# Two chained mixtures behind packed attention: the second mixture's weight sums placed later, its first output weights decoded earlier

## The chip, the cores and the metric

One core of a Trainium2 chip runs the whole program in one launch. The metric is device time in microseconds (us), lower is better. The time before is 807.88 us, the median of 3 runs (807.45 to 808.22).

## The reference

Inputs are q, k, v of shape (4, 8, 576, 64) and p of shape (4, 8, 32, 64), and two pairs of weights, `w_in` (512 x 2048) and `w_out` (2048 x 512).

```python
def sm_attn(qq, kk, vv):
    s = scale * np.matmul(qq, kk.transpose(0, 1, 3, 2))
    a = np.exp(s - np.max(s, axis=-1, keepdims=True))
    a = a / (np.sum(a, axis=-1, keepdims=True) + 1e-09)
    return np.matmul(a, vv)
p_packed = sm_attn(p, k, v)
x = sm_attn(q, p_packed, p_packed)           # as 2304 tokens x 512
h = x @ moe_w_in;  x = (h * np.tanh(softplus(h))) @ moe_w_out
h = x @ moe2_w_in; out = np.where(h > 0, h, np.exp(h) - 1) @ moe2_w_out
```

The result is 2304 x 512. The weights arrive as 64-bit numbers, so that each of them has to be decoded on the chip from two 32-bit words.

## The kernel before

Every large product is made from a high and a low part of each operand (`split_hi` on ScalarE, `split_lo` on VectorE), three matmuls for one. The engines are TensorE (PE), VectorE (DVE), ScalarE (ACT), GpSimd (POOL, here a DMA queue) and SyncE (SP, the other DMA queue). An engine works in the order in which the program gives it its instructions; outside the startup a planner orders them for each engine by its own estimate of when they are ready, with the order of the Python program as the priority. Buffers come from pools with a fixed number: `slot` (28), `small` (9), `wo` (2), `dec` (3), `sg` (2, for raw weights of the second mixture and for two of the four `yr` tiles).

**Startup.** Attention of the first two batches and the first two blocks (0 to 31) of the first mixture, in an order written out by hand.

**First mixture**, `mixture1` (L1062), iterations `i` from 32 to 129. An iteration has `gemm1(i)` (L657, six matmuls of 288 columns), `mish(i)` (L672: `t` on ACT, `gh` on ACT, `gl` on DVE) and `gemm2(i - 2)` (L691, twelve matmuls, which needs that `gl`). Into these are woven:
- the attention of batches 2 and 3, one step or two an iteration. Batch 2 starts with iteration 35, batch 3 with 65, and that of batch 3 takes some 23 iterations and the folds that come between. `packed` (L477) makes `pv` on DVE, which PE transposes; scores go through ACT's exponent (`e`);
- the folds (L625) of the packed keys into `w_in`, four for each batch, for batch 3 in iterations 87 to 92;
- the weight sums of the second mixture, `combine` (L273). That mixture's first layer is multiplied with seven products in place of eight, and for this sums and differences of the quarters of `w_in` are made ahead. There are eight `combine`s of 28 steps: two raw tiles are loaded (512 KB each on SP) and decoded (`s0` on ACT, three DVE instructions, L214, L224, L230, into `dec`), four sums are made on DVE (L282), and then there are seven pairs: `hi` on ACT into a tile `w2c` (L257), `lo` on DVE (L265) and two DMAs of 128 KB on POOL to `w2_dr` in HBM (L314), `w_dr` in the trace. The tile `w2c` comes from the two `wo` buffers and is free when both of its DMAs have landed.

`STG=(34, 110)` spreads the 224 steps evenly over iterations 34 to 109, 2.95 an iteration. At `Y0 = 114` four `yr` tiles (the tokens, from HBM) are loaded by twelve DMAs, and 36 steps of the tokens' sums (`y_steps`, L742) are spread over iterations 115 to 127. In iterations 127 to 129 the first six products of the second mixture are started.

**Second mixture**, `mixture2` (L1148): three passes over 768 tokens, each of eight quartets. A quartet (L816) has seven `product`s (L790, six matmuls of 384 columns, with `w2c` read back from HBM three tiles ahead), an ELU for four results on ACT and DVE, and four `gemm4` (L868) of nine matmuls of 512 columns. `gemm4` needs `w_out` decoded as `w2oh` and `w2ol`: for the first two quartets rows 0 to 3, for the next two rows 4 to 7, and so on. A decoding has six steps: `s0` on ACT (L194), three on DVE, `s4` on ACT (`w2oh`, L257) and `s5` on DVE (`w2ol`, L265). Before, all sixteen of them are made in `mixture2`: two ahead of its loop by `tick(14)`, then three steps behind each product in the first pass (four in the last quartet of a pass).

Of the kernel before, what the change touches and what calls it, by code (L numbers as in the profile page):

```python
# [10 lines left out]
F32R = mybir.dt.float32r  # L11
# [16 lines left out]
    EXPS=(0, 1, 2, 3, 4, 5, 6, 7, 8, 9, 10, 11, 12, 23, 24, 25, 26),  # L28
    LOW=(2, 4, 7, 9, 10, 11, 12, 13, 14, 15, 16, 17, 19, 22, 29, 30, 31),
    HALVED=True,  # L30
    STG=(34, 110),
    Y0=114,
    AHEAD=3,
)

# [31 lines left out]
def kernel(  # L67
# [202 lines left out]
        split_hi(val, hi, factor)  # L270
        split_lo(val, hi, lo, factor)

    def combine(c, p):  # L273

        tiles = [decode("w2i", 2 * p + x, c) for x in range(2)]
        d = {}

        def cut(x, h):
            return tiles[x][1]().bitcast(F32)[:, 256 * h:256 * h + 256]

        def op(out, a, b, alu):
            nc.vector.tensor_tensor(out=out(), in0=a(), in1=b(), op=alu)  # L282

        def s1():
            d["s"] = dp.tile([128, 512], I32, tag="dec", name="sums").bitcast(F32)
            op(lambda: d["s"][:, 0:256], lambda: cut(0, 1), lambda: cut(1, 1), ALU.add)

        def s2():
            op(lambda: d["s"][:, 256:512], lambda: d["s"][:, 0:256], lambda: cut(0, 0), ALU.subtract)

        def s3():
            op(lambda: cut(0, 1), lambda: cut(0, 0), lambda: cut(0, 1), ALU.subtract)

        def s4():
            op(lambda: cut(1, 0), lambda: cut(1, 0), lambda: d["s"][:, 256:512], ALU.subtract)

        vals = [
            lambda: cut(0, 0), lambda: d["s"][:, 256:512], lambda: cut(1, 0), lambda: d["s"][:, 0:256],
            lambda: cut(0, 1), lambda: cut(1, 0), lambda: cut(1, 1),
        ]  # L300

        def parts(x):
            def view():
                return vals[x]().rearrange("p (i n) -> p i n", i=2)

            def hi():
                d[x] = wo.tile([128, 2, 2, 128], F32R, tag="wo", name="w2c")
                split_hi(view(), d[x][:, :, 0, :], 1.0 / WSCALE)

            def lo():  # L310
                split_lo(view(), d[x][:, :, 0, :], d[x][:, :, 1, :], 1.0 / WSCALE)
                for i in range(2):
                    n = (2 * c + i) * 7 + x
                    nc.gpsimd.dma_start(out=w2_dr[n // 2][:, n % 2, p], in_=d[x][:, i].bitcast(F32))  # L314

            return [hi, lo]

        st = tiles[0][0] + tiles[1][0] + [s1, s2, s3]
        for x in range(7):
            if x == 5:  # L320
                st.append(s4)
            st += parts(x)
        return st
# [721 lines left out]
    class Track:  # L1045
# [11 lines left out]
        def start(self, i):  # L1057
            if not self.cur and self.q and self.q[0][0] <= i:
                self.cur = deque(self.q.popleft()[1])
                self.cur.popleft()()  # L1060

    def mixture1():  # L1062
        att, fol = Track(), Track()

        def whole(f):
            return [f[0], lambda: [f[i]() for i in (1, 3, 2, 4)]]

        at = {}
        dec = deque()
        for b in range(1, B):  # L1070
            i0 = (b - 1) * 2 * NK
            if b > 1:
                for st_ in attention_steps(b):
                    att.q.append((i0 + (3 if b == 2 else 1), st_))
                for x in range(2):
                    at.setdefault(max(i0 - 2 + 2 * x, 2 * NK), []).append(lambda b=b, x=x: load_kt(k, kt_in, b, x, "k"))
            for c in range(4):
                if b > 1 or c >= P["F1"]:
                    fol.q.append((max(i0 + NK + 4 * c + P["FOLDOFF"][c], 2 * NK), whole(fold(b, c))))
                    at.setdefault(max(i0 + NK + 4 * c + P["RELOFF"], 2 * NK), []).append(lambda c=c: reload_w1i(c))  # L1080
        w2q = deque()
        for c in range(4):
            for p_ in range(2):
                w2q.append(((2 * p_, c), (2 * p_ + 1, c)))
        cur = deque()
        ahead = deque(t for g in w2q for t in g)

        def step_w2():
            if not cur and w2q:
                if len(ahead) == 16:  # L1090
                    for _ in range(2):
                        load_raw("w2i", *ahead.popleft())
                (r, c), _ = w2q.popleft()
                st = combine(c, r // 2)
                for n in (4, 9):
                    if ahead:
                        st.insert(n, lambda t=ahead.popleft(): load_raw("w2i", *t))
                cur.extend(st)
            if cur:
                cur.popleft()()  # L1100

        for i in range(2 * NK, NA + LAG):
            for f in at.get(i, ()):
                f()
            fol.posts()
            att.posts()
            if not fol.cur and not att.cur:
                fol.start(i)
            if i < NA:
                gemm1(i)  # L1110
                for f in mish(i):
                    f()
            if 48 <= i < 64:
                att.posts()
                if not fol.cur and not att.cur and not fol.due(i):
                    att.start(i)
            for f in gemm2(i - LAG):
                f()
            if not fol.cur and not att.cur:
                fol.start(i)  # L1120
            if not fol.cur and not att.cur and not fol.due(i):
                att.start(i)
            u0, u1 = P['STG']
            if u0 <= i < u1:
                n = 8 * 28
                for _ in range((i + 1 - u0) * n // (u1 - u0) - (i - u0) * n // (u1 - u0)):
                    step_w2()
            if i == u1:
                while cur or w2q:
                    step_w2()  # L1130
            if i == P['Y0']:
                for k_ in range(4):
                    load_y(0, k_)
                ys = deque(f for st in y_steps(0) for f in st)
                n_y = len(ys)
            if P['Y0'] < i < NA:
                n = n_y * (i - P['Y0']) // (NA - 1 - P['Y0'])
                while len(ys) > n_y - n:
                    ys.popleft()()
            if i >= NA - 1 and not steps:  # L1140
                st, groups = quartet(0, 0)
                steps.extend(st)
                first.extend(groups)
            if i >= NA - 1:
                for _ in range(2):
                    steps.popleft()()

    def mixture2():  # L1148
        w2o = [4 * c + r for c in range(4) for r in (0, 2, 1, 3)]
        load = deque(w2o)  # L1150
        todo = deque()
        for _ in range(2):
            load_raw("w2o", load.popleft(), 0)

        def refill():
            r, d = w2o.pop(0), []

            def step(i):
                if not d:
                    d.extend(decode("w2o", r, 0))  # L1160
                d[i]()

            todo.extend(lambda i=i: step(i) for i in range(6))
            if load:
                todo.append(lambda r=load.popleft(): load_raw("w2o", r, 0))

        def tick(n):
            while n and todo:
                todo.popleft()()
                n -= 1  # L1170

        for _ in range(2):
            refill()
        tick(14)
        for _ in range(2):
            refill()
        ready = deque()
        for j in range(3):
            for q in range(NQ):
                lastq = q == NQ - 1 and j < 2  # L1180
                if j == 0 and q in (0, 2, 4):
                    for _ in range(4):
                        refill()
                if q == 0 and j == 0:
                    st, groups = list(steps), list(first)
                else:
                    st, groups = quartet(j, q)
                if j < 2 and q == NQ - 2:
                    for k_ in range(4):
                        load_y(j + 1, k_)  # L1190
                    ys = y_steps(j + 1)
                    todo.extend(ys[0] + ys[1])
                done = 7 - len(st)
                for x in range(7):
                    if x >= done:
                        st[x - done]()
                    if lastq and x < 5:
                        todo.extend(ys[x + 2])
                    if x in (0, 2, 4, 6):
                        if x == 6:  # L1200
                            ready.append(groups[0])
                        if ready:
                            gemm4(*ready.popleft())
                    tick(4 if lastq else 3)
                ready.extend(groups[1:])
        while ready:
            gemm4(*ready.popleft())
# [37 lines left out]
```

## Time and profile before

| | |
|---|---|
| median of 3 runs | 807.88 us |
| profiled execution, its own time | 809.47 us |
| its span | 807.5 us |
| PE busy | 758.6 us (94%) |
| PE loading weights | 676.5 us (84%) |
| DVE busy | 534.1 us (66%) |
| ACT busy | 398.0 us (49%) |
| mean granted PE clock | 0.973 |

The profile shows one execution, in microseconds from the start of its span. An engine that is not the bound may idle at no cost; what counts is where PE stops, what ended its stop, and at which clock it works. "<-" names the releaser of a wait: the instruction or the DMA that ended it. A DMA has an issue (the time that its queue needs for it) and a landing (from the issue to the arrival of the data). Iteration 32 of the loop begins at 126.96 us, iteration 84 at 292.73, 96 at 328.86, 112 at 369.12 and 117 at 380.95; the last block's `gemm1` ends at about 405.10 us, and at 444.00 the second mixture runs on without stops. Cutting the windows there gives the stretches of the change.

### The profile page before, as it was taken

What the parts mean: (1) busy time and instruction counts of PE and PEld (TensorE: products, weight loads), DVE (VectorE), ACT (ScalarE), POOL (GpSimd) and SP (SyncE); (2) the same over time, 40 slices, a digit from 0 to 9 for tenths busy, and PEclk for the clock granted to TensorE, in tenths of its full rate; (3) what the DMA queues carried; (4) which work ended last, traced back from release to release, by engine and by line L of the source; (5) the groups of instructions that cost most, each with busy time, mean ns of one, the idle gap of its engine ahead of it and who ended that gap; (6) DMA issues with size and microseconds to landing.
All of it is one profiled execution on the core that took longest, in us unless ns stands there. A gap on an engine that the chain in (4) does not pass through costs nothing.

```text
span 807.5 us, 14023 instructions
## 1 busy us (share of the span) xinstructions
PE 758.6 (94%) x5237; PEld 676.5 (84%) x5237; DVE 534.1 (66%) x1134; ACT 398.0 (49%) x840; POOL 76.0 (9%) x145
## 2 busy tenths in 40 slices
PE   6399999986999899999987999999999999999997
PEld 4198898875888898999976989888899999888986
DVE  5999977553974579565357988686446667454644
ACT  2899734562764547545444544354223345322323
POOL 1100001222133223321000000000000000000000
PEclk9599999998999999999997999999999999999999
DMA  8998455667356654472245526455443437443412
GB/s 296 413 365 264 125 151 227 208 174 223 130 169 236 165 183 162 150 235 96 105 175 184 192 79 207 132 200 163 147 115 120 117 106 227 138 130 106 126 57 78
DMA packets 79299, 138.80 MB, mean 172 GB/s; under 512 B 38528, under 2 KB 46720, under 8 KB 79232
## 3 DMA queue, kind: packets, MB, share of 16 engines
q1 hardware_dynamic: 69984, 112.55, 43.7%
q0 software_dynamic: 7808, 23.60, 7.8%
q10 hardware_dynamic: 1440, 1.77, 0.7%
q8 instruction: 41, 0.67, 0.3%
q14 instruction: 26, 0.21, 0.1%
HBM read 109.58 MB, written 28.31 MB: 171 GB/s over the span
## 4 chain that ended last, share of the span: by engine, by line
PE 67%; DVE 10%; ACT 9%; DMA 8%; issue 4%; SPq 1%; POOL 0%; ACTq 0%; DVEq 0%
PE h L799 19%; PE o L879 7%; PE o L880 7%; PE o L881 7%; PE acc L703 5%; PE acc L705 5%; DMA w_dr<-w2c 5%; PE acc L704 5%; PE h L667 3%; PE h L668 2%; PE h L669 2%; PE pm L633 1%; DMA yr<-y_dr 1%; ACT t L677 1%; DVE dec L224 1%
## 5 line engine op out<-in xcount | busy, mean ns | idle before, releaser
L799 PE MATMUL h<-y,w2c 128*128 128x384 f32 x1008 | 199.1, 339 | 4.6 <-ACT hs L376 3.4
L799 PEld LDWEIGHTS h<-y,w2c 128*128 128x128 f32 x1008 | 180.7, 189 | 16.4 <-ACT hs L376 3.8
L703 PE MATMUL acc<-gh,w1oh 128*128 128x288 f32 x512 | 151.3, 301 | 2.9 <-DVE y L378 2.0
L705 PE MATMUL acc<-gh,w1ol 128*128 128x288 f32 x512 | 152.4, 299 | 0.0
L704 PE MATMUL acc<-gl,w1oh 128*128 128x288 f32 x512 | 152.3, 299 | 0.1
L879 PE MATMUL o<-w2oh,gh 128*128 128x512 f32 x288 | 114.6, 399 | 4.6 <-ACT w2oh L257 3.9
L880 PE MATMUL o<-w2ol,gh 128*128 128x512 f32 x288 | 113.5, 394 | 0.0
L703 PEld LDWEIGHTS acc<-gh,w1oh 128*128 128x128 f32 x512 | 96.8, 191 | 10.7 <-issue 6.7
L881 PE MATMUL o<-w2oh,gl 128*128 128x512 f32 x288 | 102.2, 395 | 0.0
L705 PEld LDWEIGHTS acc<-gh,w1ol 128*128 128x128 f32 x512 | 97.7, 191 | 3.5 <-issue 3.4
L704 PEld LDWEIGHTS acc<-gl,w1oh 128*128 128x128 f32 x512 | 97.8, 191 | 3.0 <-issue 1.8
L685 DVE TENSOR_TENSOR gl<-t,gh 128x288 fp32r<-128x288 f32 x128 | 57.2, 451 | 44.7 <-ACT gh L376 43.6
L667 PE MATMUL h<-a2h,gh 128*128 128x288 f32 x256 | 78.2, 306 | 5.8 <-ACT t L677 4.5
L677 ACT ACTIVATE t<-h 128x288 f32<-128x288 f32 x128 | 50.9, 403 | 52.6 <-PE h L669 52.3
L668 PE MATMUL h<-a2l,gh 128*128 128x288 f32 x256 | 76.3, 299 | 0.0
L669 PE MATMUL h<-a2h,gl 128*128 128x288 f32 x256 | 76.1, 299 | 0.0
L314 POOL DMA_DIRECT2D w_dr<-w2c x112 | 60.0, 541 | 164.1 <-DVE w2c L265 156.2
L257 ACT ACTIVATE gh<-t 128x384 fp32r<-128x384 f32 x96 | 50.1, 523 | 47.9 <-DVE t L810 46.5
L879 PEld LDWEIGHTS o<-w2oh,gh 128*128 128x128 f32 x288 | 54.6, 190 | 15.0 <-ACT w2oh L257 4.2
L263 DVE TENSOR_TENSOR gl<-t,gh 128x384 fp32r<-128x384 f32 x96 | 52.9, 553 | 15.2 <-ACT gh L257 14.7
L880 PEld LDWEIGHTS o<-w2ol,gh 128*128 128x128 f32 x288 | 54.6, 190 | 9.7 <-DVE w2ol L265 0.2
L376 ACT ACTIVATE gh<-t 128x288 fp32r<-128x288 f32 x112 | 49.4, 443 | 26.0 <-PE acc L705 23.9
(128 smaller groups left out, 1050.5 us busy)
## 6 DMA issues: line engine op xcount, KB each, us to landing
w2c<-w_dr SPq DMA_DIRECT2D x84, 512.0 KB, 3.7
w_dr<-w2c POOLq DMA_DIRECT2D x112, 128.0 KB, 2.6
w1r<-w_dr SPq DMA_DIRECT2D x24, 512.0 KB, 6.6
raw_w1i<-in_moe_w_in_dram SPq DMA_DIRECT2D x16, 512.0 KB, 10.7
raw_w1o<-in_moe_w_out_dram SPq DMA_DIRECT2D x16, 512.0 KB, 9.3
raw_w2i<-in_moe_w_in_dram SPq DMA_DIRECT2D x16, 512.0 KB, 4.4
raw_w2o<-in_moe_w_out_dram SPq DMA_DIRECT2D x16, 512.0 KB, 3.4
y_dr<-y POOLq DMA_DIRECT2D x16, 288.0 KB, 2.8
```

Of the source, the lines that this page charges most:

```text
L314: nc.gpsimd.dma_start(out=w2_dr[n // 2][:, n % 2, p], in_=d[x][:, i].bitcast(F32))
L667: nc.tensor.matmul(out=hp, lhsT=wh, rhs=xh, start=(kt == 0), stop=False)
L668: nc.tensor.matmul(out=hp, lhsT=wh, rhs=xl, start=False, stop=False)
L669: nc.tensor.matmul(out=hp, lhsT=wl, rhs=xh, start=False, stop=(kt == 1))
L677: nc.scalar.activation(out=d["t"], in_=d["h"], func=ACTF.Mish)
L703: nc.tensor.matmul(out=o, lhsT=wh[:, cs], rhs=gh, start=first, stop=False)
L704: nc.tensor.matmul(out=o, lhsT=wh[:, cs], rhs=gl, start=False, stop=False)
L705: nc.tensor.matmul(out=o, lhsT=wl[:, cs], rhs=gh, start=False, stop=last)
L799: nc.tensor.matmul(out=hp, lhsT=w[:, p, a, :], rhs=y[:, b, :], start=start and p == 0 and i == 0, stop=p == 1 and i == 2, skip_group_check ...
L879: nc.tensor.matmul(out=o, lhsT=gh[:, ts], rhs=wh, start=(n == 1), stop=False)
L880: nc.tensor.matmul(out=o, lhsT=gh[:, ts], rhs=wl, start=False, stop=False)
L881: nc.tensor.matmul(out=o, lhsT=gl[:, ts], rhs=wh, start=False, stop=(n == NK))
```

## The change

The even spread becomes two: 70 steps over iterations 32 to 83, and 154 over iterations 84 to 111 (5.5 an iteration). The third number of a stretch is its steps. In the second stretch `w2c` comes from the nine `small` buffers, two pairs sharing one tile, in place of the two `wo` buffers. The first group of `w_out` (rows 0, 2, 1, 3) is loaded and decoded from iteration 112 on, 28 steps at six an iteration; the tokens' sums start with `Y0 = 117` and are spread over 118 to 127. The other three groups are queued with quartets 0, 2 and 4 as whole groups, and two steps in place of three follow each product.

```diff
-    STG=(34, 110),
-    Y0=114,
+    STG=((32, 84, 70), (84, 112, 154)),
+    W0=112,
+    Y0=117,
...
-    def combine(c, p):
+    def combine(c, p, late):
...
             def hi():
-                d[x] = wo.tile([128, 2, 2, 128], F32R, tag="wo", name="w2c")
+                if not late:
+                    d[x] = wo.tile([128, 2, 2, 128], F32R, tag="wo", name="w2c")
+                else:
+                    if x % 2 == 0:
+                        d["w"] = small([128, 2, 2, 2, 128], F32R, "w2c")
+                    d[x] = d["w"][:, x % 2]
                 split_hi(view(), d[x][:, :, 0, :], 1.0 / WSCALE)
...
+    todo = deque()
+
+    def second(c):
+        rows = [4 * c + r for r in (0, 2, 1, 3)]
+        for r in rows[:2]:
+            todo.append(lambda r=r: load_raw("w2o", r, 0))
+        for x, r in enumerate(rows):
+            d = []
+
+            def step(i, r=r, d=d):
+                if not d:
+                    d.extend(decode("w2o", r, 0))
+                d[i]()
+
+            todo.extend(lambda i=i, step=step: step(i) for i in range(6))
+            if x < 2:
+                todo.append(lambda r=rows[x + 2]: load_raw("w2o", r, 0))
+
+    def tick(n):
+        while n and todo:
+            todo.popleft()()
+            n -= 1
...
-            u0, u1 = P['STG']
-            if u0 <= i < u1:
-                n = 8 * 28
-                for _ in range((i + 1 - u0) * n // (u1 - u0) - (i - u0) * n // (u1 - u0)):
-                    step_w2()
-            if i == u1:
+            for u0, u1, n in P['STG']:
+                if u0 <= i < u1:
+                    for _ in range((i + 1 - u0) * n // (u1 - u0) - (i - u0) * n // (u1 - u0)):
+                        step_w2(u0 > 2 * NK)
+            if i == P['STG'][-1][1]:
                 while cur or w2q:
-                    step_w2()
+                    step_w2(True)
+            if P['W0'] <= i < P['Y0']:
+                if i == P['W0']:
+                    second(0)
+                tick(28 // (P['Y0'] - P['W0']) + 1)
             if i == P['Y0']:
+                tick(28)
                 for k_ in range(4):
                     load_y(0, k_)
...
     def mixture2():
-        w2o = [4 * c + r for c in range(4) for r in (0, 2, 1, 3)]
...
-        for _ in range(2):
-            refill()
-        tick(14)
-        for _ in range(2):
-            refill()
...
                 if j == 0 and q in (0, 2, 4):
-                    for _ in range(4):
-                        refill()
+                    second(q // 2 + 1)
...
-                    tick(4 if lastq else 3)
+                    tick(4 if lastq else 2)
```

## Rows read from the trace of the kernel before

**Rows 1.** Busy time by stretch: length, PE, PEld, DVE, ACT, POOL, PE clock, DMA share, GB/s.
```profile
126.96:292.73 165.77, 152.02 (x1367) 133.83 (x1366) 98.95 (x224) 88.68 (x203) 41.31 (x77) 0.97 0.57 179
292.73:328.86 36.13, 36.13 (x315) 31.88 (x314) 32.82 (x72) 23.62 (x50) 9.72 (x19) 1.00 0.55 186
328.86:369.12 40.26, 39.45 (x307) 38.22 (x305) 20.41 (x46) 20.18 (x50) 14.24 (x27) 1.00 0.55 185
369.12:380.95 11.83, 11.83 (x92) 11.83 (x91) 5.72 (x13) 6.16 (x16) 1.17 (x3) 1.00 0.32 117
380.95:405.10 24.15, 24.15 (x185) 24.15 (x185) 10.70 (x24) 12.45 (x30) 0.00 (x0) 1.00 0.23 88
405.10:444.00 38.90, 31.09 (x151) 27.47 (x150) 26.07 (x50) 17.31 (x32) 1.08 (x2) 0.87 0.52 185
```

**Rows 2.** Waits of PE from 126.96 to 405.10: total, times, longest.
```profile
PE pm L517 <- DVE pv L500: 4.0, 1, 4.0
PE h L667 <- ACT t L677: 3.9, 6, 1.2
PE pm L460 <- ACT e L433: 3.0, 2, 2.1
PE acc L703 <- DVE y L378: 2.0, 1, 2.0
PE acc L703 <- ACT gh L376: 0.9, 1, 0.9
PE pm L411 <- ACT e L433: 0.4, 1, 0.4
```

**Rows 3.** Timeline of ACT, then DVE, near 190 us: start, length, instruction, idle before.
```profile
190.54 0.42 ACT L257 ACTIVATE w2c<-dec 128x256 fp32r<-128x256 f32 x1 [3.77 <-DMA w_dr<-w2c]
...
190.99 0.42 DVE L265 SCALAR_TENSOR_TENSOR w2c<-dec,w2c 128x256 fp32r<-128x256 f32 x1 [5.31 <-ACT w2c L257]
```

**Rows 4.** Waits of ACT from 126.96 to 405.10, the row of the writes.
```profile
ACT w2c L257 <- DMA w_dr<-w2c: 37.4, 16, 3.8
```

**Rows 5.** Tile `w2c` in 127 to 370 us, last line in 292.73 to 328.86.
```profile
L314 POOL DMA_DIRECT2D w_dr<-w2c x112: 539/539/702, 136.5 to 368.7; - x112
...
DMA to landing us min/median/max: 2.0/2.6/10.6
...
DMA to landing us min/median/max: 2.0/2.4/4.5
```

**Rows 6.** Timeline of ACT, DVE and SP: a `t`, its `gl`, the loads `yr`.
```profile
396.30 0.41 ACT L677 ACTIVATE t<-h 128x288 f32<-128x288 f32 x1 [1.49 <-PE h L669]
...
397.22 0.46 DVE L685 TENSOR_TENSOR gl<-t,gh 128x288 fp32r<-128x288 f32 x1 [1.92 <-ACT gh L376]
...
346.16 6.92 SPq L739 DMA_DIRECT2D yr<-y_dr  x12
```

**Rows 7.** Waits of PE from 405 to 445.
```profile
PE o L879 <- ACT w2oh L257: 3.9, 1, 3.9
PE h L799 <- ACT hs L376: 3.4, 1, 3.4
```

**Rows 8.** Busy time in the four stretches of half clock, columns as in rows 1.
```profile
194.16:200.98 6.82, 5.57 (x23) 5.54 (x23) 2.21 (x5) 0.02 (x1) 2.13 (x4) 0.50 0.38 141
269.25:272.66 3.41, 3.41 (x16) 3.41 (x15) 2.95 (x7) 1.90 (x5) 0.00 (x0) 0.50 0.61 96
422.85:429.67 6.82, 5.14 (x12) 4.04 (x13) 4.78 (x9) 2.93 (x5) 0.00 (x0) 0.50 0.63 241
439.92:443.33 3.41, 3.27 (x11) 2.77 (x10) 3.32 (x6) 2.20 (x5) 0.00 (x0) 0.50 0.70 227
```

**Rows 9.** DVE on tile `dec` by stretch: length, busy (x), PE clock, DMA share, GB/s.
```profile
126.96:369.12 242.16, 57.71 (x120) 0.98 0.57 181
292.73:328.86 36.13, 12.98 (x27) 1.00 0.55 186
405.10:444.00 38.90, 15.30 (x26) 0.87 0.52 185
```

More of the change, by code (lines that the diff above doesn't have):

```diff
@@ L1086, in mixture1, with step_w2 @@
         ahead = deque(t for g in w2q for t in g)
-        def step_w2():
+        def step_w2(late):
             if not cur and w2q:
@@ L1093, in step_w2 @@
                 (r, c), _ = w2q.popleft()
-                st = combine(c, r // 2)
+                st = combine(c, r // 2, late)
                 for n in (4, 9):
@@ L1148, in mixture2 @@
     def mixture2():
-        w2o = [4 * c + r for c in range(4) for r in (0, 2, 1, 3)]
-        load = deque(w2o)
-        todo = deque()
-        for _ in range(2):
[L1153 to L1170, printed above, removed]
-        for _ in range(2):
-            refill()
-        tick(14)
-        for _ in range(2):
-            refill()
         ready = deque()
```

## The prediction

> **What bounds the kernel now.** I read first the windows of the middle of the run, cut at iterations of the first mixture's loop, to see how much of each stretch TensorE (PE) works [rows 1]. In iterations 32 to 83 PE is busy 152.02 of 165.77 us at a mean clock of 0.97; from 84 to 127 it hardly idles; at the hand-over to the second mixture it is busy 31.09 of 38.90 us at 0.87. So PE is the bound, and what can be won lies in two places: iterations 32 to 83 and the hand-over. VectorE (DVE) shows the other side: 32.82 of 36.13 us busy in iterations 84 to 95, half busy in 96 to 111, 10.70 of 24.15 us in 117 to 127.
>
> Second, PE's own waits in the loop [rows 2]: 14.2 us. The longest, 4.0 us for `pv` of the attention, is followed back in two rows [rows 3]: DVE, which makes `pv`, stood 5.31 us at the low part of a weight sum; that waited for ScalarE (ACT), which had stood 3.77 us until an earlier write of such a sum had landed. ACT did that 16 times, 37.4 us in all [rows 4]: there are two `wo` buffers, and each is free only when two POOL issues of 539 ns and their landing (2.0 to 10.6, median 2.6 us) are over [rows 5]. A burst of sums goes at 224/76 = 2.95 steps an iteration, and two sums are four steps: a buffer comes round every 1.36 iterations of 2.38 us (1.92 + 0.46 between two `gl` [rows 6]) = 3.2 us. Low part, issues and landing take 0.4 + 1.1 + 2.6 = 4.1 us. So ACT must wait.
>
> Third, the hand-over: PE idles 3.9 us for the first `w2oh` and 3.4 us for `hs`, which stands on ACT behind four more weight decodings [rows 7]. Last, the clock: four stretches at 0.5, that is 1.2 GHz, each after such a stop [rows 8].
>
> **The change, part by part.** The sum is made against the profiled execution, 809.47 us (span 807.5), 1.6 us above the median of 807.88.
>
> *Early sums thinned out.* By iteration 84 the old plan issues 50 x 2.95 = 147 steps, the new one 70. At 70/52 = 1.35 steps a buffer comes round every 4/1.35 x 2.38 = 7.1 us, against the 4.1 us above; even a landing of 5 us is met. Of the waits of [rows 2] I put 4.0 (`pv`), 2.0 (`y`), 0.9 (`gh`), 0.4 (the scores) and half of the 3.9 (`t`, made by the same ACT queue) to those landings: 9.3, of which I take 8.7. To decodings that stood on DVE ahead of the attention's maximum I put 3.0 (`e`) and a quarter of `t`: 4.0, and with half the steps half stays, 2.0 won. The last quarter of `t` stays. Clock: PE worked 5.57 us in the stretch at 194 us, which costs 2.8; the stop before it goes, so all of that. The stretch at 269 us costs 3.41/2 = 1.7; its stop is of the decoding kind, so half, 0.85. **Won: 8.7 + 2.0 + 2.8 + 0.9 = 14.4** (bounds 4, if the attention's own chain is what holds, and 17.8, if everything goes).
>
> *First weights decoded ahead.* The four decodings for the first quartets leave the hand-over. The idles of 3.9 and 3.4 us go, and the half clock, where PE worked 5.14 and 3.27 us [rows 8], gives back 2.6 + 1.6. That is 11.5. Late next: the second group's decodings, 14 steps in program order before the seventh product, on the same DVE. The first `gemm4` needs none of them, so I leave 1.5 us. **Won: 10.0** (bounds 2 and 11.5). Two steps a product in place of three afterwards: the 28 steps of a group fill its 14 products exactly; I cost it at nothing, covered by those products; uncovered, the first `gemm4` of the next group would wait one decoding.
>
> *Sums behind the last attention.* DVE pays 57.71 us for 120 instructions on `dec` [rows 9], and 16 low parts from `sums` at 0.42 [rows 3]: 64.4 us, 8.0 for each of the eight sums. In iterations 84 to 95 the old run did 12.98 us on `dec` [rows 9] and 3 x 0.42, 14.2 us of it; 12 x 5.5 = 66 steps of 28 are 2.36 sums, 18.9 us. DVE then needs 32.82 + 4.7 = 37.5 of 36.13 us. This is the tight place. What queues behind a late DVE instruction is `gl`, for which `gemm2` waits. Slack: `t` starts when PE releases it, `gl` ends 1.38 us later [rows 6], `gemm2` comes two iterations (4.76 us) later: 3.4 us. The excess and half of DVE's idle, 1.4 + 1.7 = 3.1 us, fit just so; I charge 2.0 (bounds 0 and 7). In 96 to 111 DVE takes the rest, 3.14 sums or 25.2 us, in place of some 10 of its 20.41: 36 of 40.26, no cost. POOL issues 14 x 0.54 = 7.5 us a sum, 5.5 sums or 42 us in 76; it is free for that. The late tiles come from the nine `small` buffers; the attention takes its `x` and `a2t` there until about iteration 92, and behind an allocation that waits for a landing of 2.4 us [rows 5] stands again DVE. That lies within the bound of 7.
>
> For these writes the row shows no sign of a busy DVE: in iterations 84 to 95, with DVE at 32.82 of 36.13 us, they land in 2.0 to 4.5, median 2.4 us [rows 5], against 2.6 in the loop as a whole. The Trainium skill, SBUF — State Buffer, section "SBUF: two separate sides", speaks against the change here: while DVE runs an instruction in a mode with both ports, GpSimd cannot write the descriptors of a DMA that it issues. The trace does not bear it out; by it the denser stretch would lose what rival 4 works out, 7 us.
>
> *Four decodings in iterations 112 to 116.* They cost DVE 4 instructions each, 15.30/26 x 4 = 2.35 us [rows 9], so 9.4; with the 5.72 there now (an upper bound, since some of it is tokens' sums that move on) 15.1 of 11.83 us: 3.3 over, about the slack. I charge 1.0 (bounds 0 and 3.3). *Tokens' sums start at 118, not 115.* SP's twelve loads of `yr` take 6.92 us to issue [rows 6], and the first two tiles can be loaded only when the raw weights have left their two buffers; before, they were issued at 346.16 us, long before iteration 114 (112 begins at 369.12). ACT may then stand at a `y` with `t` behind it: I charge 1.5 (bounds 0 and 4); from 117 on DVE has 13 us free. **Lost: 2.0 + 1.0 + 1.5 = 4.5.**
>
> Sum: 14.4 + 10.0 - 4.5 = 19.9. The profiled execution would be 789.6, the median **788.0 us**.
>
> **The rivals.**
> 1. *DVE becomes the bound behind the last attention.* No slack absorbs anything: 4.7 in 84 to 95 (its idle of 3.3 stays), 3.3 in 112 to 116, 2.5 for low parts that wait for ACT in between, one half-clock stretch 1.7: 12.2 in place of 4.5 with the loads' stop left out, so 24.4 - 12.2 = 12.2: 795.7 us. For it: 32.82 of 36.13. Against: PE did not stop there at all.
> 2. *The attention's waits stay*, since its own chain (scores, exponent, transposes) is as long as before. 4 won in place of 14.4: 9.5, 798.4 us. Against: [rows 3].
> 3. *The change does not do what it says*: the planner orders every engine, and the decodings may slip back behind the tokens' sums. The hand-over gives 2: 11.9, 796.0 us.
> 4. *POOL's writes are held up by DVE.* Each issue waits for one DVE instruction, 15.30/26 = 0.59 us [rows 9]: 14 x 1.13 = 15.8 us a sum against 76.4/5.5 = 13.9 that are there, so writes are 10.5 us late by iteration 112 and hold buffers that the decodings want; less the slack of 3.4, 7 us: 12.9, 795.0 us. Against: [rows 5]. The Trainium skill's page named above would have it so.
> 5. *Rivals 1 and 2 together*: 4 + 10 - 12.2 = 1.8: 806.1 us, at the edge of what can be told.
> 6. *Slower.* What moves is 77 steps, 77/28 x 8.0 = 22.0 us, and 9.4 us of decoding: 31.4 us of DVE work between iterations 84 and 116. If PE waits for all of it, since `gl` is queued behind it and `gl` is on PE's path, that is 31.4 against 24.4 won: 814.9 us. It decides from 24.4/31.4 = 78% of the moved work on the path. For it: the DVE is a FIFO, as [rows 3] show. Against: the free third of DVE from 96 on.
>
> **How the numbers follow.** Forecast 0.53, rivals 1 to 6: 0.18, 0.11, 0.05, 0.03, 0.03, 0.07. A measurement can tell 0.2% (1.6 us) from no change. Faster by more: forecast and rivals 1 to 4, 0.90; rival 5 counts as within, 0.03; slower 0.07. The forecast's own range: with everything won and nothing lost 17.8 + 11.5 = 29.3, 778.6 us; with 10 and 7 won and 7 lost, 797.9 us. Rivals 1 to 4 lie between 795.0 and 798.4; with some 2.6 us of error on the last, the range is 779 to 801. Outside are rivals 5 and 6 and the tails, less than 0.2.
>
> **What would show it.** Right: ACT's waits for `w_dr<-w2c` fall from 37.4 to under 10 us; PE's 4.0 us at `pv` is gone and no half clock follows that attention; at the hand-over PE goes from the seventh product into the first `gemm4` with less than 1.5 us idle, at full clock; iterations 84 to 111 last about 76 us as now with DVE near 36 of 36 in the first 36. Wrong: PE waiting for `gl` between iterations 84 and 117 by more than 5 us (rivals 1, 6), landings of `w_dr` over 4 us there (rival 4), `w2oh` decoded after the tokens' sums (rival 3), or a `pv` or `e` wait of 2 us and more with ACT not at a `w2c` (rival 2).

## The result and the profile after

The changed kernel takes **783.37 us** (median of 4 runs, 782.44 to 785.86) against 807.70 us for the kernel before, run beside it: ratio **0.9703**, 95% interval 0.9679 to 0.9726. The profiled execution took 782.82 us, its span 781.0, so 26.5 us of span are won. In the changed kernel the line numbers are larger by 1 in the decodings (`w2c` in 258 and 266) and by 6 from `w2_dr`'s DMA to the second mixture's products (`t` in 683, `gl` in 691, products in 805).

The page's busy line and PE's clock in 40 slices:

```profile
PE 749.5 (96%) x5237; PEld 669.6 (86%) x5237; DVE 529.9 (68%) x1134; ACT 397.1 (51%) x840; POOL 75.9 (10%) x145
...
PEclk9699999999999999999999999999999999999999
```

PE ran the same 5237 matmuls in 9.1 us less busy time (758.6 before), and idled 31.5 us in place of 48.9. The four stretches at a granted clock of 0.5 (1.2 GHz) [rows 8] are gone. They held 5.57, 3.41, 5.14 and 3.27 us of work at half speed, which costs half of that, 8.7 us: this is nearly all of the 9.1. The other 17.4 us are stops of PE.

The same stretches as in [rows 1], cut at the same iterations 32, 84, 96, 112, 117 and 127, then the hand-over:

```profile
127.21:276.81 149.60, 146.77 (x1372) 130.30 (x1371) 84.94 (x188) 80.64 (x181) 22.63 (x43) 1.00 0.52 154
276.81:313.46 36.65, 36.51 (x310) 31.39 (x309) 30.41 (x69) 24.53 (x54) 13.29 (x26) 1.00 0.58 192
313.46:352.61 39.15, 39.15 (x307) 38.15 (x306) 32.98 (x80) 27.07 (x68) 25.12 (x47) 1.00 0.77 258
352.61:361.35 8.74, 8.74 (x69) 8.74 (x67) 6.11 (x12) 5.33 (x13) 5.36 (x11) 1.00 0.80 250
361.35:386.02 24.67, 24.41 (x185) 24.12 (x184) 19.80 (x42) 16.63 (x40) 0.00 (x0) 1.00 0.73 256
386.02:425.00 38.98, 38.01 (x215) 34.96 (x214) 23.32 (x50) 17.27 (x34) 1.08 (x2) 1.00 0.56 187
```

Iterations 32 to 83 take 149.60 us in place of 165.77. Iterations 84 to 111 take 75.8 in place of 76.4, though of the 112 writes of weight sums 77 are now issued from iteration 84 on, in place of 42. From iteration 112 to the end it is 428.4 against 438.4 (in the two kernels 2186 matmuls each; how many of these fall before iteration 127 differs, so the cut at 127 compares nothing). Sum: 16.2 + 0.6 + 10.0, less 0.25 by which iteration 32 began later.

Waits of PE from 127 to 386 us, then from 386 to 430, and the row of the writes among ACT's waits of 127 to 385:

```profile
PE h L673 <- ACT t L683: 2.0, 3, 1.4
PE acc L709 <- ACT gh L382: 0.8, 1, 0.8
PE acc L710 <- DVE gl L691: 0.3, 1, 0.3
...
PE h L805 <- ACT hs L382: 0.6, 1, 0.6
PE h L805 <- DVE t L816: 0.4, 1, 0.4
...
ACT w2c L258 <- DMA w_dr<-w2c: 14.6, 7, 3.8
```

The stops for `pv`, `e`, `y` and the scores of [rows 2] are gone, as are the 3.9 and 3.4 us of [rows 7]. ACT's stand for landings has fallen from 37.4 us [rows 4], but only to 14.6. The timeline of ACT shows why any is left (start, length, instruction, idle before it):

```profile
156.50 0.42 ACT L258 ACTIVATE w2c<-sums 128x256 fp32r<-128x256 f32 x1 [3.35 <-DMA w_dr<-w2c]
...
217.09 0.42 ACT L258 ACTIVATE w2c<-sums 128x256 fp32r<-128x256 f32 x1 [3.59 <-DMA w_dr<-w2c]
224.25 0.42 ACT L258 ACTIVATE w2c<-dec 128x256 fp32r<-128x256 f32 x1 [3.81 <-DMA w_dr<-w2c]
```

The prediction's "a buffer comes round every 7.1 us" is a mean. Pairs of a `combine` come close behind one another, and landings go beyond their median: these three stands, 10.8 of the 14.6 us, wait for writes that took up to 6.8, 3.2 and 5.1 us to land. So within a sum ACT still meets the ring of two. 12.3 of the 14.6 us lie in iterations 32 to 83, 2.3 behind them.

### The profile page after: what moved, and what is told of

It reads as the page before. It is cut to its first block, busy times and chain, and to the rows that moved or that the text cites. A ratio compares the mean times of both kernels' runs of the same rounds, so it can differ in the third digit from the quotient of the medians.

```text
span 781.0 us, 13981 instructions
## 1 busy us (share of the span) xinstructions
PE 749.5 (96%) x5237; PEld 669.6 (86%) x5237; DVE 529.9 (68%) x1134; ACT 397.1 (51%) x840; POOL 75.9 (10%) x145
## 4 chain that ended last, share of the span: by engine, by line
PE 76%; DVE 7%; ACT 7%; DMA 5%; issue 3%; POOL 1%; ACTq 0%; SPq 0%; DVEq 0%; POOLq 0%
PE h L805 22%; PE o L885 8%; PE o L887 8%; PE o L886 8%; PE acc L710 5%; PE acc L709 5%; PE acc L711 5%; DMA w_dr<-w2c 3%; PE h L673 3%; PE h L674 3%; PE h L675 3%; PE pm L639 1%; PE pm L491 1%; POOL w_dr L320 1%; ACT t L683 1%
## 5 line engine op out<-in xcount | busy, mean ns | idle before, releaser
L710 PE MATMUL acc<-gl,w1oh 128*128 128x288 f32 x512 | 150.7, 296 | 0.5 <-DVE gl L691 0.3
L711 PE MATMUL acc<-gh,w1ol 128*128 128x288 f32 x512 | 150.1, 295 | 0.0
L709 PE MATMUL acc<-gh,w1oh 128*128 128x288 f32 x512 | 148.5, 297 | 0.8 <-ACT gh L382 0.8
L709 PEld LDWEIGHTS acc<-gh,w1oh 128*128 128x128 f32 x512 | 94.8, 188 | 8.2 <-issue 5.2
L710 PEld LDWEIGHTS acc<-gl,w1oh 128*128 128x128 f32 x512 | 96.1, 188 | 4.7 <-issue 1.8
L887 PE MATMUL o<-w2oh,gl 128*128 128x512 f32 x288 | 100.0, 393 | 0.0
L711 PEld LDWEIGHTS acc<-gh,w1ol 128*128 128x128 f32 x512 | 96.1, 188 | 0.9 <-issue 0.8
L675 PE MATMUL h<-a2h,gl 128*128 128x288 f32 x256 | 76.4, 300 | 0.0
```

What stands on the lines that cost most here:

```text
L675: nc.tensor.matmul(out=hp, lhsT=wl, rhs=xh, start=False, stop=(kt == 1))
L709: nc.tensor.matmul(out=o, lhsT=wh[:, cs], rhs=gh, start=first, stop=False)
L710: nc.tensor.matmul(out=o, lhsT=wh[:, cs], rhs=gl, start=False, stop=False)
L711: nc.tensor.matmul(out=o, lhsT=wl[:, cs], rhs=gh, start=False, stop=last)
L887: nc.tensor.matmul(out=o, lhsT=gl[:, ts], rhs=wh, start=False, stop=(n == NK))
```

## The experiments

Lengths of stretches of the profiled executions, in us; 84 to 111 is one column, 112 to the end another. "Early" and "late" are the steps in iterations up to 83 and 84 to 111; "2", "3" and "nine" are the buffers of the tiles `w2c`, two `wo` early and nine `small` late where nothing is said (before and in e2 two `wo` for all). Iteration 32, ahead of every edit, begins between 126.75 and 128.67 us in these executions, so about 2 us of a span is the startup's own spread.

| kernel | early/late | median us | ratio (interval) | 32–83 | 84–111 | 112–end |
|---|---|---|---|---|---|---|
| before | even, 34–109 | 807.70 | 1 | 165.8 | 76.4 | 438.4 |
| changed | 70/154 | 783.37 | 0.9703 (0.9679–0.9726) | 149.6 | 75.8 | 428.4 |
| e1 | 70/154 | 793.42 | 0.9827 (0.9802–0.9852) | 149.0 | 75.8 | 439.2 |
| e2 | even | 798.17 | 0.9891 (0.9860–0.9923) | 164.9 | 75.3 | 427.5 |
| e4 | even, 3 buffers | 798.84 | 0.9898 (0.9875–0.9922) | 156.2 | 74.6 | 438.5 |
| e3 | 70/154, 2 for all | 808.29 | 1.0023 (1.0006–1.0039) | 150.8 | 76.9 | 452.7 |
| e5 | 0/224 | 818.77 | 1.0127 (1.0099–1.0156) | 146.5 | 91.0 | 454.3 |
| e6 | 70/154, 3 steps | 786.82 | 0.9732 (0.9710–0.9755) | 149.6 | 75.8 | 432.2 |
| e7 | 70/154, 3 buffers | 782.37 | 0.9673 (0.9651–0.9695) | 146.5 | 76.6 | 429.9 |
| e9 | 42/182 | 800.34 | 0.9904 (0.9877–0.9931) | 151.5 | 81.5 | 435.7 |
| e10 | 42/182, e1's decoding | 802.20 | 0.9931 (0.9910–0.9953) | 151.2 | 81.2 | 440.3 |
| e8 | 98/126, nine for all | 780.59 | 0.9663 (0.9644–0.9681) | 147.2 | 76.8 | 427.5 |
| e11 | 98/126, nine for all | 780.23 | 0.9651 (0.9623–0.9680) | 147.0 | 76.8 | 426.1 |
| e12 | 126/98, nine for all | 779.63 | 0.9645 (0.9618–0.9671) | 148.1 | 75.4 | 428.3 |

**e1 and e2: the change cut in two.** e1 places the sums as the change does and decodes `w_out` in `mixture2` as before. e2 keeps the even spread and decodes ahead.

```diff
 e1 (against the changed kernel; mixture2 as before)
-    Y0=117,
+    Y0=114,
...
-                    tick(4 if lastq else 2)
+                    tick(4 if lastq else 3)
 e2 (against the changed kernel; all w2c from wo)
-    STG=((32, 84, 70), (84, 112, 154)),
+    STG=((34, 110, 224),),
```

> Only the placement of the weight sums: 70 steps in iterations 32 to 83 and 154 in 84 to 111, these in the small buffers; the output weights are decoded in the second mixture as before, tokens' sums from iteration 114. Theory (two places, each with its own gain): iterations 32 to 83 shorten by 14 to 18 us, 84 to 111 stay within 2 us of 76.4, the hand-over keeps its two stops of 3.9 and 3.4 us: 790 to 793 us. Rival (DVE is the bound behind the last attention, and only the early decoding's other effects hide it): 84 to 111 takes over 81 us and the time is over 796. Rival (the gain came from the hand-over): over 800.

> Only the early decoding: the 224 steps of the sums are spread evenly over iterations 34 to 109 in the two wo buffers as before; the first group of output weights is decoded in 112 to 116, two steps a product afterwards. Theory: the stops of 4.0 us at pv and the like stay, the hand-over loses its two stops and its half clock: 10 to 12 us won, 796 to 798 us; together with the run of the placement alone the two gains add up to the whole of 24 us. Rival (the gains are not independent, the decoding only pays when the sums are out of the way): under 7 us won, over 801 us.

Waits of PE in e1 from 388.92 to 430 us:

```profile
PE h L805 <- ACT hs L382: 3.9, 1, 3.9
PE o L885 <- ACT w2oh L258: 3.9, 1, 3.9
```

Waits of PE in e2 from 126.75 to 386 us, and ACT's row of the writes there:

```profile
PE pm L523 <- DVE pv L506: 4.0, 1, 4.0
PE h L673 <- ACT t L683: 3.1, 4, 1.7
PE pm L466 <- ACT e L439: 3.0, 2, 2.1
PE acc L709 <- DVE y L384: 2.0, 1, 2.0
...
ACT w2c L258 <- DMA w_dr<-w2c: 28.6, 15, 4.0
```

Each half removes its own stops and leaves the other's in place, and both times lie within half a microsecond of what the theory expected. The product of the two ratios is 0.9827 x 0.9891 = 0.9720, inside the interval of the whole: the parts hardly touch each other. Placement is worth about 14 us, decoding ahead about 9.

**e3 and e4: what the buffers do.** e3 takes the late tiles from the two `wo` buffers too. e4 is the kernel before with a third `wo` buffer (a constant, `one`, goes into a `dec` buffer to make room).

```diff
 e3 (against the changed kernel)
-                        step_w2(u0 > 2 * NK)
+                        step_w2(False)
...
-                    step_w2(True)
+                    step_w2(False)
 e4 (against the kernel before)
-    wo = ctx.enter_context(tc.tile_pool(name="wo", bufs=2))
+    wo = ctx.enter_context(tc.tile_pool(name="wo", bufs=3))
...
-            one = const.tile([128, 128], F32R, name="one")
+            one = dp.tile([128, 512], F32R, tag="dec", name="one")[:, 0:128]
```

> The changed kernel, but with the two wo buffers for all sums. Theory (the landing of the writes sets the pace of a two-buffer ring): in iterations 84 to 111 a buffer would have to come round every 4/5.5 x 2.38 = 1.7 us and needs 4.1 (0.4 low part, 1.1 issues, 2.6 landing), so ACT stands for landings by 40 us and more in that stretch and t of the first mixture comes late: 84 to 116 grows by 5 to 20 us, 788 to 803 us. Rival (the buffers do not matter, the slack of 3.4 us and the planner's order hide the waits): within 2 us of the changed kernel, 782 to 785 us.

> The kernel before with three wo buffers in place of two and nothing else of the change (a small constant of the startup is moved into another pool to make room). Theory (the stops of the attention come from the ring of two): a buffer comes round every 6/2.95 x 2.38 = 4.8 us against the 4.1 that it needs, so ACT's waits for landings fall from 37.4 to under 20 us, the 4.0 us at pv goes with its half clock, and 6 to 11 us are won, 797 to 802 us. Rival (the number of steps beside the attention matters, not their buffers: DVE and ACT are too full there): the pv stop or another of its size stays, under 3 us won, over 804 us.

e3 loses the whole gain, but not where it was looked for. The stretch 84 to 111 is only 1.1 us longer; the price stands behind 112. Waits of PE from 385 to 430 us, and the timeline of SP:

```profile
PE h L805 <- ACT y L258: 14.4, 2, 14.0
PE h L805 <- ACT hs L382: 2.7, 1, 2.7
```

```profile
381.17 19.33 SPq L156 DMA_DIRECT2D raw_w2o<-in_moe_w_out_dram  x3
...
409.53 1.34 SPq L745 DMA_DIRECT2D yr<-y_dr  x3
413.13 1.27 SPq L745 DMA_DIRECT2D yr<-y_dr  x3
```

With two buffers the last write is issued at 409.0 us in place of 356.4. Behind the late sums the raw `w_out` tiles get their two buffers late, behind these the last two `yr` tiles (409.5 to 414 us), behind these the tokens' sums, and PE waits for a `y` for 14 us and then works 23.9 us at half clock. So the nine buffers are what lets 154 steps end in time. That the pair of `sg` buffers for raw weights and `yr` carries the delay on is read from this order; a third one was not tried.

e4, waits of PE from 127.39 to 370 us, and ACT's row of the writes:

```profile
PE pm L460 <- ACT e L433: 3.1, 2, 1.6
PE h L667 <- ACT t L677: 2.8, 4, 1.4
PE acc L703 <- DVE y L378: 1.7, 1, 1.7
...
ACT w2c L257 <- DMA w_dr<-w2c: 20.1, 12, 3.4
```

A third buffer alone takes away the `pv` stop and both half-clock stretches of the loop: 9.6 of the 16.2 us. `e` and `y` stay. Ahead of both `e` stops ACT stood 2.3 and 2.5 us for a decoding on DVE (at 168.32 and 255.77 us), so these were not the ring's. For `y` this is not shown: 7 us before that copy ACT had stood 3.18 us for a landing and DVE 3.14 us behind it. Of the early stretch 6.6 us are left that the changed kernel does not have. Thinning takes them away there, but it is not shown to be the only way: e12 below makes 126 of some 147 steps early from nine buffers, without these stops (148.1 us). The even spread with nine buffers was not run.

**e5, e9, e10: how full the late stretch may be.**

```diff
 e5
-    STG=((32, 84, 70), (84, 112, 154)),
+    STG=((84, 112, 224),),
 e9 (and e10: the same line in e1)
-    STG=((32, 84, 70), (84, 112, 154)),
+    STG=((32, 84, 42), (84, 112, 182)),
```

> All 224 steps of the sums in iterations 84 to 111 (8 an iteration), none before. DVE then needs 22 us more than the changed kernel's 73.2 of 75.8 us in that stretch. Theory (the price of too many sums is not paid where DVE is full, since gl has slack and the planner lets the sums fall behind, but at the hand-over: sums end late, so the raw output weights, the tokens' tiles and the tokens' sums come late, as in the run with two buffers): the last write of sums comes 15 to 25 us later than 356 us, PE waits under 4 us between iterations 84 and 117, and over 4 us at the first products of the second mixture with a half clock after it: 788 to 800 us. Rival (PE waits for gl, because DVE's queue is a FIFO): over 15 us of waits for gl or t in 84 to 117. Rival (DVE has room enough later): within 2 us of 783.

> 42 steps in iterations 32 to 83 and 182 in 84 to 111 (6.5 an iteration): one sum, 8 us of DVE, more in the late stretch. Theory: the sums end 5 to 8 us later than 356 us, the tokens' tiles still land before iteration 122, and the time stays within 2 us of the changed kernel, 781.5 to 785.5, perhaps 1 us better for the stops left in the early stretch. Rival (the late stretch is full to the brim, every further sum shows): 787 us and more.

> One more sum is moved behind the attention (42 steps ahead, 182 behind), with the first output weights decoded in the second mixture as in the kernel before. With those weights decoded ahead, the same placement cost 17 us more than 70 and 154 did. Theory A, that the decodings of the weights, queued on DVE between the late sums and the accumulators' copies `y` of the last block, make that price: without them one more sum behind the attention costs little, so 793 to 797 us, as the run of the placement alone (793.4), iterations 96 to 111 about 40 us. Theory B, that the late sums alone fill DVE: iterations 96 to 111 again take 44 us and the sums spill into 112 to 126; the time is that of the placement alone plus 12 to 17, 805 to 811 us.

e5 is slower than before, by 1.3%, far outside the theory's 788 to 800 us. Its waits of PE from 300 to 450 us:

```profile
PE acc L709 <- DVE y L384: 18.9, 2, 18.1
PE h L673 <- ACT t L683: 9.5, 2, 6.5
PE acc L710 <- DVE gl L691: 2.2, 2, 2.0
```

The 18.1 us come at the change from block 6 to 7 of the first mixture (iteration 112), where DVE copies the accumulators to `y`: the copy is queued behind the last sums and the decodings of `w_out`. The hand-over, where the price was expected, pays nothing. (The expectation's 73.2 us of DVE in the changed kernel are wrong: 30.41 + 32.98 = 63.4 of 75.8.)

e9 puts a single sum more behind the attention and loses some 16 us of the 24 (0.0201 x 808); its rival came, not its theory. e10 tells what part the decodings have in it: without them the same step costs 0.0104 x 808 = 8.4 us, measured from e1. So neither theory holds alone. Up to iteration 112 both kernels lose the same 7.5 us (1.9 + 5.7 in e9, 2.1 + 5.4 in e10); behind it e9 loses another 7.3, e10 only 1.1. The latter part is e5's mechanism; waits of PE in e9 from 361 to 407 us:

```profile
PE acc L709 <- DVE y L384: 3.7, 2, 1.9
PE h L673 <- ACT t L683: 1.8, 1, 1.8
```

Of the former part some 2 us lie in iterations 32 to 83, the rest mostly in 96 to 111. Windows of e10, iterations 96 to 111, columns as in [rows 1]; then the waits of ACT there; then the timelines of ACT and PE near 323 us:

```profile
316.41:360.28 43.87, 40.78 (x307) 38.40 (x305) 35.17 (x88) 28.48 (x76) 28.14 (x53) 1.00 0.77 256
```

```profile
ACT raw_w2i L195 <- DMA raw_w2i<-in_moe_w_in_dram: 8.1, 4, 2.2
ACT w2c L258 <- DVE dec L231: 7.8, 6, 2.4
```

```profile
322.01 0.66 ACT L195 ACTIVATE raw_w2i<-raw_w2i 128x512 f32<-128x512 f32 x1 [2.22 <-DMA raw_w2i<-in_moe_w_in_dram]
322.57 0.57 ACT L258 ACTIVATE gh<-pm 128x512 fp32r<-128x512 f32 x1
323.05 0.40 ACT L683 ACTIVATE t<-h 128x288 f32<-128x288 f32 x1
...
323.50 0.40 PE L673 MATMUL h<-a2h,gh 128*128 128x288 f32 x1 [1.65 <-ACT t L683]
```

DVE is busy 35.17 of 43.87 us. ACT stands 2.22 us at a decoding for its 512 KB of raw weights, `t` waits behind that, and PE stops 1.65 us for `t`. The changed kernel and e1 have no wait for `raw_w2i` in this stretch. The loads issued there land in a median of 5.7 us in e10 and 4.9 in the changed kernel, from two buffers. This is one stop: PE idles 3.1 us of the 4.7 by which the stretch is longer, 1.0 of them for `gl` from DVE. So raw loads have a part in the price, DVE is not excluded, and the rest stays open. That a third raw buffer would move this edge was not tried.

The 2 us in iterations 32 to 83, with fewer sums in them, are the ring of two once more. Both kernels have an `e` stop of 2.8 or 2.9 us there with 3.4 us of half clock behind it, and in both ACT and DVE stand for a landing just ahead of the attention's `sm`, from which `e` is made. The timelines of ACT and DVE in e10:

```profile
168.50 0.42 ACT L258 ACTIVATE w2c<-dec 128x256 fp32r<-128x256 f32 x1 [2.62 <-DMA w_dr<-w2c]
...
168.94 0.43 DVE L266 SCALAR_TENSOR_TENSOR w2c<-dec,w2c 128x256 fp32r<-128x256 f32 x1 [1.88 <-ACT w2c L258]
169.29 0.15 DVE L432 TENSOR_SCALAR sm<-sm 128x1 f32<-128x1 f32 x1
```

So at a mean of 42/52 = 0.8 early steps an iteration two buffers can still cost a stop, where a burst of pairs meets the attention.

**e6: three steps a product.** The edit of e1's last line alone.

> The changed kernel with three steps a product in the second mixture as before, in place of two. Theory (the sparser decoding there neither costs nor wins, since a group fills its products either way): within 1.5 us of the changed kernel, 782 to 785 us. Rival (the two steps make room on ACT and DVE at the hand-over, and three would put back a stop at hs): 2 us and more slower, with a PE wait for hs of over 2 us.

By the ratios 0.0029 x 808 = 2.3 us slower, with intervals that overlap (0.9679–0.9726 and 0.9710–0.9755), so a price of up to some 6 us is possible and none is shown. The three passes of e6 have no stop over 1.1 us, as the changed kernel has none over 0.7.

**e7, e8, e11, e12: a better placement.** e7 is the changed kernel with e4's third buffer. The others move the split, e8 and e12 with that third buffer and e11 without it.

```diff
 e8 and e11
-    STG=((32, 84, 70), (84, 112, 154)),
+    STG=((34, 84, 98), (84, 112, 126)),
 e12
+    STG=((34, 84, 126), (84, 112, 98)),
```

> The changed kernel with three wo buffers for the early sums. ACT still stands 14.6 us for landings in iterations 32 to 84, and PE's waits for t and gh there are 2.8 us. Theory: these go in part: 1 to 2.5 us faster than the changed kernel, 781 to 782.5 us. Rival (what is left is the folds' and the attention's own): no change, 783 to 784 us.

> The changed kernel with three early buffers and the even placement 98 and 126 (34 to 83, 84 to 111) in place of 70 and 154, to see whether the late stretch can be relieved once the early buffers come round. Theory A, that the early buffers alone were what an early step cost: with three of them 98 steps early are as cheap as 70, and the lighter late stretch gives up to 1 us: 781 to 783 us. Theory B, that an early step costs also by DVE ahead of the attention's maximum and `pv`, whatever the buffers: 28 steps more bring back `t` and `e` waits of 3 to 6 us in iterations 32 to 83, and the time is 785 to 789 us.

> The changed kernel with the placement 98 and 126 (34 to 83, 84 to 111) and its two early buffers. Theory A, the prediction's arithmetic of the ring of two: at 98/50 = 1.96 steps an iteration a buffer comes round every 4/1.96 x 2.38 = 4.9 us, against 4.1 us for low part, issues and a median landing; the waits stay gone and the time is that of the changed kernel, 782 to 785 us. Theory B, that a ring is paced by the landings above the median and by steps that come in bursts: ACT stands for landings 20 us and more again, waits of PE for `pv`, `e` or `y` of 3 us and more come back in iterations 32 to 83, and the time is 788 to 794 us, while the same placement with three buffers took 780.6.

> Three early buffers, with the placement 126 and 98. Theory A, that with three buffers the early steps cost nothing until the ring of three is full (126/50 = 2.52 an iteration, a buffer every 6/2.52 x 2.38 = 5.7 us against 4.1): 780 to 782 us. Theory B, that the attention's DVE chain pays for more early steps whatever the buffers: `t` and `e` waits of 3 us and more in iterations 32 to 83, 784 to 790 us, since the evenly spread sums with three buffers (2.95 an iteration) kept 6.6 us more in that stretch than the changed kernel.

In e8, e11 and e12 the edit does more than these expectations say. Which buffers a step uses is decided by `step_w2(u0 > 2 * NK)`, with `2 * NK` = 32, and their first stretch begins at 34 in place of 32. So the early tiles too come from the nine `small` buffers, and e8's and e12's third `wo` buffer holds no weight sum. The trace of e11 shows it; ACT, then POOL:

```profile
208.99 0.71 ACT L258 ACTIVATE w2c<-dec 128x256 fp32r<-128x256 f32 x2
209.60 0.40 ACT L258 ACTIVATE w2c<-sums 128x256 fp32r<-128x256 f32 x1
...
210.20 0.41 ACT L258 ACTIVATE w2c<-sums 128x256 fp32r<-128x256 f32 x1
210.51 0.72 ACT L258 ACTIVATE w2c<-dec 128x256 fp32r<-128x256 f32 x2
...
212.04 7.46 POOL L320 DMA_DIRECT2D w_dr<-w2c  x14 [23.85 <-DVE w2c L266]
```

Six high parts are made before the first of their writes is issued, which two or three buffers cannot hold. So e8 and e11 are the same kernel for the sums (780.59 and 780.23 us), and neither theory of e8, e11 or e12 on two or three buffers has been tested: whether two are enough at 98 early steps stays open.

With nine early buffers and 98 early steps ACT has no wait for `w_dr<-w2c` at all, and e11 has one row of waits of PE from 127 to 390 us:

```profile
PE h L673 <- ACT t L683: 2.8, 4, 1.1
```

With 126 early steps (e12) ACT stands 1.5 us for a landing, and PE stops 1.6 us for `pv`. e7 gives the changed kernel's split a third `wo` buffer: ACT's stand falls from 14.6 to 5.7 us and iterations 32 to 83 take 146.5 in place of 149.6 us, so the ring of two still costs there. The time, 782.37 us, cannot be told from the changed kernel's.

**The fastest kernel is e12, 779.63 us**, whose interval lies clear of the changed kernel's; those of e8 and e11 just touch it. Among the three nothing can be told apart. They differ from the changed kernel in two things, the split and the buffers of the early sums, and no run separates these. Beyond 154 late steps the time rises steeply (e9, e5).

## Why the prediction was right

The forecast was 788.0 us, the time 783.37; the mechanism was right in the main and the win larger than its 19.9 us. The spans put 26.5 us against it, term by term:

- **Early sums thinned out: 14.4 forecast, 16.2 measured**, under the bound of 17.8. The split inside was off. Landings with their clock were put at 8.7 + 2.8; e4, which changes the buffer alone, gives 9.6 with the clock of both stretches. "Half stays" of the decodings, 2.0 + 0.9, was too careful: the 6.6 us that e4 leaves are gone in the changed kernel. The 2.0 us of `y` were put to the landings, and e4 still shows 1.7 of them. The sign "under 10 us" for ACT's stands was missed (14.6), and the arithmetic behind it has a wrong term: 2.38 us an iteration is read near the end of the loop, while iterations 32 to 83 took 165.77/52 = 3.19 us each. With 3.19 a buffer of the old plan came round every 4/2.95 x 3.19 = 4.3 us, not sooner than the 4.1 that it needs, so on the mean ACT need not have waited at all. That the ring of two costs PE its `pv` stop is shown by e4; that the mean said so too was luck. What decides is how close pairs follow one another and how late single writes land.
- **Decoded ahead with the two losses behind it: 10.0 - 1.0 - 1.5 = 7.5 forecast, 10.0 measured** (11.0 in e2). The remaining stop was put at 1.5, and the hand-over idles 38.98 - 38.01 = 0.97 us. What was charged for the four decodings and for `yr` was not paid: from 352.61 to 386.02 us PE idles 0.26 us. It is paid as soon as the sums spill into that stretch (e9, e5, e3), so the two charges were the right places at the wrong load.
- **Two steps a product, costed at nothing**: no cost shows against the kernel before, and e6 shows no win of three. From 444 us on PE idled 6.56 us there (363.50 - 356.94), and from 425 us on it idles 7.13 now:

```profile
425.00:781.00 356.00, 348.87 (x1725) 311.74 (x1723) 223.73 (x462) 137.44 (x277) 0.00 (x0) 1.00 0.42 135
```

- **Sums behind the attention: 2.0 lost forecast, 0.6 won.** The step that failed is "DVE then needs 37.5 of 36.13 us" in iterations 84 to 95. It took 30.41 of 36.65. Two reasons show. The planner did not do there what the program's order asked: of the 33 writes of 2.36 sums 25 were issued, and 44 followed in 96 to 111. And what DVE does besides decoding fell from 32.82 - 12.98 = 19.8 us to 30.41 - 13.70 = 16.7; DVE on tile `dec`, by stretch:

```profile
276.81:313.46 36.65, 13.70 (x30) 1.00 0.58 192
313.46:352.61 39.15, 21.75 (x49) 1.00 0.77 258
```

So a share of DVE worked out from the program's order can be too high where a planner may hold work back: it filled 96 to 111 (32.98 of 39.15) with work whose due time lay behind. The slack of `gl` was also larger than the 3.4 us of the prediction, which again took 2.38 us an iteration: in 84 to 95 one took 36.13/12 = 3.01 us.

**The rivals.** 1 (DVE the bound) and 6 (slower) did not come, but they were near: one sum more costs two thirds of the gain, and two and a half more cost all of it and 10 us besides. Their place was wrong: the stops that were followed back are not at `gl` in every iteration, but at `t` behind ACT's wait for raw loads and at DVE's copy of the accumulators at the block change. 2 (the attention's own chain) falls by the changed kernel, which has no `pv` or `e` stop left; e4 already loses that for `pv`. 3 falls by the hand-over, which e1 shows with the decodings late. 4 (writes held by DVE) falls by the tile `w2c` in 127 to 370 us:

```profile
L320 POOL DMA_DIRECT2D w_dr<-w2c x112: 539/539/551, 136.1 to 356.4; - x112
...
DMA to landing us min/median/max: 2.0/3.2/6.8
```

With DVE 84% busy (32.98 of 39.15 us in iterations 96 to 111) no issue took over 551 ns. The landings did grow, to a median of 3.2 us (2.6 before [rows 5]), but with nine buffers ACT stood only 2.3 us for them in iterations 84 to 111, and PE idled 0.14 us there. The Trainium skill (SBUF — State Buffer, section "SBUF: two separate sides") says that GpSimd cannot write the descriptors of its DMA while DVE runs an instruction in a mode with both ports. Nothing like it is seen in this trace (in e12 a single issue took 939 ns, for a reason not looked into); the runs do not show whether any of these DVE instructions used the mode that it speaks of.

## What to carry to other kernels

Where PE stops for an engine that waits for a landed write, count the buffers against issue plus landing within a burst, and with the landings above the median; the mean rate is too kind, since stands came at 1.35 and at 0.8 steps an iteration. Take the length of an iteration from the stretch in question. Thinning the work out and adding one buffer are both cheap tests, and here each brought part of the same stop.

Work moved into a slack stretch is free up to an edge and may then cost more than its own length: one sum more, 8 us of DVE, cost 8 to 16 us, two and a half cost 35. It stands in in-order queues ahead of things with a fixed date, so find the edge by moving one unit more and one unit less. Before blaming the engine whose busy share is highest, look at what it and its neighbours stand for: two of the stops beyond the edge were a raw load and one copy in a queue, with DVE idle 20% of the time.

When a variant moves one number, look in its trace whether only that has changed. Here a start at 34 in place of 32 also changed the buffers.

## What was not expected of the hardware

Landings of the same 128 KB write had a median of 2.4 us in iterations 84 to 95 before, where DMA was busy 55% [rows 5]; in iterations 84 to 111 of the changed kernel, at 58 to 77%, it was 3.3 us. The busy share of DMA does not order them: in the same iterations e11 had 2.3 us at 59 to 66%, and e12 3.4 us at 50 to 60%. What orders them stays open. No stretch of half clock follows the changed kernel's longest stop in the loop, 1.4 us for `t`, while in e10 a stop of 2.80 us for `e`, which ends at 171.94 us, is followed by 3.4 us of it. In e9 stops of 1.8 and 1.9 us, which end at 369.50 and 376.36 us, are followed by it too.
